# The first product of each iteration placed inside the older iteration's second product

## The chip, the cores and the metric

One of the eight cores of one Trainium2 chip runs the whole problem. The metric is the device time of one execution in microseconds (us). The engines are TensorE (PE in the profile; PEld are its weight loads), VectorE (DVE), ScalarE (ACT), GpSimd (POOL) and SyncE (SP, which here issues the DMAs).

## The reference

A softmax over 7 taps for each row and head, a causal mix of 7 neighbouring rows with these weights, and a feed-forward layer with `h * cos(h)` in the middle:

```python
w = exp(weight_gen - max); w = w / (sum(w) + 1e-09)      # (8, 4096, 8 heads, 7)
out = einsum('bshk,bskhg->bshg', w, x_unf)               # 7 rows of x, 192 columns
h = x @ w_in                                             # x = out as (32768, 192); w_in (192, 2048)
g = h * cos(h)
return g @ w_out                                         # w_out (2048, 192)
```

## The kernel before

The 32768 rows are cut into 64 blocks of 512. For each block GpSimd makes the mixed rows `xa` (`attention`, L257 products and L272 sums), TensorE transposes them (L316 for the steady part, L307 for the first blocks), ScalarE and GpSimd split them into a high part `x_hi` (L297) and a low part `x_lo` (L299). The feed-forward layer is computed in such high and low parts throughout.

The 2048 hidden columns are 8 "pairs" of 256. The main loop runs over i = 0 to 518, and i = 8b + pair names one block b and one pair. **One iteration** records:

- for i, the first product `x @ w_in` into one of 3 PSUM buffers `h`: `ffn_in_first` (L337, 6 slots of TensorE) and `ffn_in_second` (L354, 12 slots). The two halves of TensorE's rows write to two banks, and trade them between the two functions;
- for i − 1 and i − 2, the cosine and the split of g on ScalarE and VectorE: `act_turns` (L364), `dve_fraction` (L368), `act_cos` (L372), `dve_g` (L375), `act_hi` (L382), `dve_lo` (L386, which frees the h buffer);
- for j = i − 6, a part of the second product `g @ w_out`: `ffn_out` (L416), 16 slots with the high part `ghi` in f32, two transposes (L316), then 16 slots with the low part `glo` in bf16. Its `rest` picks a part of these: `False` all but the last 8 bf16 slots, `True` these last 8, `None` everything.

Two iterations in a row, j even and j odd, sum into one accumulator `acc`, and there is a single buffer for it (`ps_m`, `bufs=1`). After the odd one ScalarE copies it to SBUF (`evacuate`, L439; L443 where it holds no transposes), and only then may the next even one start. The same copy brings out the transposed rows.

Each engine runs its instructions in the order in which the code records them; the last loop of the kernel fixes that order. On ScalarE an iteration is L364, L382, L372, the split of x (L297), then the copy L439. Between `ffn_in_first` and `ffn_in_second`, and between the two iterations of an accumulator, `traded` puts a wait on SyncE's queue (shown in the profile under L283), so that the trade of banks is in order; L354 waits for it.

Every 32 iterations a softmax for 4 blocks runs beside this. Its exponential on ScalarE, with two loads of function tables, comes at `step == EXP`. In the iteration after it (`early_sums`) the products are recorded ahead of `act_hi`, and in the three after that (`EXP + 2 <= step <= EXP + 4`, i = 32, 33, 34, then 64, 65, 66 and so on) L337 stands between the two parts of `ffn_out`. In all other iterations `ffn_in_first` comes first, then the whole `ffn_out`, then `ffn_in_second`. For the first blocks (i = 5 and 13) a whole block is transposed in one go, and `ffn_out` comes before `ffn_in_first`. In iterations 1 to 8 parts of the weights are still being split (`two_parts`, L130 to L146), which takes h buffers too (`make_room`).

Of the kernel before, what the change touches and what calls it, by code (L numbers as in the profile page):

```python
# [43 lines left out]
def tile_softmax_conv_then_cos_ffn(  # L44
# [70 lines left out]
    def make_room():  # L115
        sizes = ps_h.tile([P, 2, CT], F32, name="h")
        bits = work.tile([P, 2, CW], F32, name="t1", tag="turn", bufs=TMP)
        room[:] = [(sizes[:, n, 0:CW].bitcast(I32), bits[:, n, :].bitcast(I32)) for n in range(2)]
# [68 lines left out]
    def softmax(r0, r1, eng, early=True, to=None):  # L187
        n = (r1 - r0) * H
        if r0 == 0:
            t = const.tile([P, n, K], F32, name="taps0")  # L190
        else:
            tile_ = work.tile([P, RW * H, K], F32, name="taps")
            t = tile_[:, 0:n, :]
        nc.sync.dma_start(out=t.rearrange("p a k -> p (a k)"), in_=g_v[:, :, r0 * H * K:r1 * H * K])
        for b in range(r0 // R, r1 // R):
            taps[b] = t.rearrange("p (r h) k -> p r h k", h=H)[:, b * R - r0:(b + 1) * R - r0]
        yield
        top_ = work.tile([P, RW * H], F32, name="top")
        top = top_[:, 0:n]
        nc.vector.tensor_reduce(out=top, in_=t, axis=AX.X, op=ALU.max)  # L200
        yield
        eng.tensor_tensor(
            out=t, in0=t, in1=top.unsqueeze(2).broadcast_to([P, n, K]), op=ALU.subtract)
        yield
        nc.scalar.activation(out=t, in_=t, func=AF.Exp)
        yield
        den_ = work.tile([P, RW * H], F32, name="den")
        den = den_[:, 0:n]
        if early:
            nc.vector.tensor_reduce(out=den, in_=t, axis=AX.X, op=ALU.add)  # L210
        else:
            add_taps(t, den)
        (nc.vector if early else nc.gpsimd).tensor_scalar(
            out=den, in0=den, scalar1=1e-9, scalar2=TWO_PI, op0=ALU.add, op1=ALU.mult)
        yield
        nc.vector.reciprocal(out=den, in_=den)
        yield
        m = 0 if to is None else to.shape[1]
        if m:
            eng.tensor_tensor(  # L220
                out=to, in0=t[:, 0:m], in1=den[:, 0:m].unsqueeze(2).broadcast_to([P, m, K]), op=ALU.mult)
        eng.tensor_tensor(
            out=t[:, m:], in0=t[:, m:], in1=den[:, m:].unsqueeze(2).broadcast_to([P, n - m, K]),
            op=ALU.mult)
        ready.update(range(r0 // R, r1 // R))
# [76 lines left out]
    def transpose_all(b):  # L302
        xa = mixed[b]
        tr = ps_h.tile([P, 2, CT], F32, name="h")
        for part in range(2):
            for r in range(R):
                nc.tensor.transpose(tr[:, part, r * P:(r + 1) * P], xa[:, r, columns(part)], ident)  # L307
        transposed.add(b)
        return tr
# [51 lines left out]
    def act_turns(i):  # L361
        t = work.tile([P, 2, CT], F32, name="turn", bufs=TMP)
        turns[i] = t
        nc.scalar.activation(out=t.bitcast(I32), in_=hs[i], func=AF.Identity, bias=0.25, scale=1.0)  # L364
# [27 lines left out]
    def ffn_out(j, rest=None):  # L392

        b, m = divmod(j, 2 * R)
        half, m = divmod(m, R)
        tp, s = divmod(m, 2)
        group = j // 2
        if s == 0 and not rest:  # L400
            accs[group] = ps_m.tile([P, 2, CT], F32, name="acc")
        acc = accs[group]
        whole = j + LAG >= N
        for lo in range(2):
            for c in range(2 * HALF):
                if rest is not None and rest != (lo == 1 and c >= HALF):
                    continue
                pair, n = divmod(c, 2)
                g = g_parts[b * NPAIR + half * HALF + pair][lo]
                fc = half * 2 * HALF + c  # L410
                for q in range(1 if whole else 2):
                    rs = slice(0, P) if whole else slice(q * D2, (q + 1) * D2)
                    bank = q ^ s
                    t = 2 * tp + bank
                    to, w = (acc[:, bank, 0:2 * D], wo) if lo == 0 else (acc[:, bank, 0:D], wo_b)
                    nc.tensor.matmul(  # L416
                        to, lhsT=g[rs, n, t * P:(t + 1) * P], rhs=w[rs, fc, :],
                        start=(lo == 0 and c == 0 and (whole or s == 0)),
                        stop=(lo == 1 and c == 2 * HALF - 1 and (whole or s == 1)),
                        skip_group_check=True)  # L420
            if lo == 0 and not rest:
                bt = group // R + 2
                if WHOLE < bt < NB:
                    transpose_row(bt, group % R, acc, s)
        if s == 0 and not whole and rest is not False:
            traded(acc)
# [60 lines left out]
    def until_mixed(b):  # L487
        while b not in mixed_all:
            next(bg)


    def all_of(*steps):
        steps = list(steps)
        while steps:
            steps = [s for s in steps if next(s, steps) is not steps]
# [71 lines left out]
    N = NB * NPAIR  # L567

    sm = sm2
    EXP = 6  # L570
    SOFTMAX = (0, 2, 3, EXP, 7, 12, 13)
    for i in range(N + LAG + 1):
        b, pair = divmod(i, NPAIR)
        j = i - LAG
        step = i % (SB * NPAIR) - (SB - 1) * NPAIR
        if step < 0 and i >= SB * NPAIR:
            step += SB * NPAIR
        if step == 0 and b + 4 < NB:
            r0 = (b + 4) * R
            sm = softmax(r0, min(r0 + RW, RPP), nc.gpsimd, early=False)  # L580
        busy = b + 4 < NB if step < NPAIR else b + 3 < NB
        exps = busy and step == EXP
        converts_now = converts.get(i, ())
        if converts_now:
            make_room()

        whole = None
        if pair == TR and b + 1 <= WHOLE:
            until_mixed(b + 1)
            whole = transpose_all(b + 1)  # L590
        if 0 <= j and j % (2 * R) == 0 and WHOLE < j // (2 * R) + 2 < NB:
            until_mixed(j // (2 * R) + 2)

        def products():
            if b < NB and pair == 0:
                assert b in transposed
            if whole is not None and j >= 0:

                ffn_out(j)
                ffn_in_first(i, whole)  # L600
            elif busy and EXP + 2 <= step <= EXP + 4:

                ffn_out(j, rest=False)
                ffn_in_first(i)
                ffn_out(j, rest=True)
            else:
                if i < N:
                    ffn_in_first(i, whole)
                if j >= 0:
                    ffn_out(j)  # L610
            if i < N:
                ffn_in_second(i)
            if j in stores:
                stores.pop(j)()
            if j >= 0:
                evacuate(j)


        early_sums = busy and step == EXP + 1
        if 0 <= i - 1 < N:  # L620
            act_turns(i - 1)
        if early_sums:
            products()
        if 0 <= i - 2 < N:
            act_hi(i - 2)
        all_of(*converts.pop(i - 1, ()))
        if exps:
            next(sm)
        now, later = [], []
        if not (busy and EXP + 1 <= step <= EXP + 3):  # L630
            now = list(splits)
            splits.clear()
        if whole is not None:
            t = work.tile([P, 2, CT], F32, name="part0", bufs=3)
            nc.scalar.copy(out=t, in_=whole)
            later.append(split(b + 1, t, slice(0, CT), nc.vector))
        if 0 <= i - 1 < N:
            dve_fraction(i - 1)
            act_cos(i - 1)
        for c in now:  # L640
            next(c)
        splits.extend(later)
        if 0 <= i - 2 < N:
            dve_lo(i - 2)
        if 0 <= i - 1 < N:
            dve_g(i - 1)
        for _ in range(4):
            for c in converts_now:
                next(c)
        all_of(*now)  # L650
        if i == N + LAG:
            break
        if not early_sums:
            products()
        load_weights(i)
        if step in SOFTMAX and step != EXP or NPAIR - 2 <= i < NPAIR + 1:
            next(sm, None)
        for _ in range(3 if i < 12 or i < 64 and i % 4 == 0 else 2):
            next(bg, None)
# [41 lines left out]
```

## Time and profile before

| | |
|---|---|
| median of 3 runs | 2300.2 us (2299.84 to 2303.83) |
| span of the profiled execution | 2300.3 us |
| TensorE busy | 2215.2 us |
| GpSimd, VectorE, ScalarE busy | 2002.3, 1905.0, 1897.5 us |
| DMA | 105.55 MB, mean 46 GB/s |

The profile is of one execution; its span lies within the runs' times. Its page gives totals by engine and slice, and its groups by line. The list of waits says who waited for whom, how long in total, how often and for how long at most. The timeline lists instructions in the order of time; in it "x2" are two slots that follow each other, and the number in brackets is the engine's idle time ahead and what ended it. Consecutive slots of TensorE overlap, so its steps are read from start to start.

### The profile page before, as it was taken

Reading aid. Unit: us, or ns where it says so; the run is one execution under the profiler, and the core shown is the slowest. Engines: PE = TensorE matmul, PEld = TensorE weight load, DVE = VectorE, ACT = ScalarE, POOL = GpSimd, SP = SyncE. Lnnn points to the kernel's source line nnn. Section 1 sums busy time; section 2 is a strip of 40 time slices with the busy share of each in tenths; the row PEclk is TensorE's granted clock in tenths of the full one; section 3 lists DMA queues with packets and bytes.
Section 4 is the critical chain, followed back from the end, with each engine's and each line's share of the span. In section 5 each row is a group of like instructions: output and inputs, shape, how many; then the busy total and the mean of one; then the engine's idle time right before and its main releaser. Section 6 shows DMA issues by size and latency. Waiting matters only on the chain.

```text
span 2300.3 us, 60609 instructions
## 1 busy us (share of the span) xinstructions
PE 2215.2 (96%) x26504; PEld 1993.6 (87%) x26504; DVE 1905.0 (83%) x1646; ACT 1897.5 (82%) x2131; POOL 2002.3 (87%) x1461
## 2 busy tenths in 40 slices
PE   3799999999999999999999999999999999999998
PEld 2588998889888888998989988898888889899897
DVE  7788888888888888888888888888888888888886
ACT  4588888888888888888888888888888888888885
POOL 8699989999999989989899899989989899899840
PEclk8799999999999999999999999999999999999999
DMA  6211221211211211211211212212211212212100
GB/s 154 56 43 40 50 51 33 58 41 34 58 39 44 50 40 44 50 49 34 58 33 43 58 31 52 50 32 52 50 41 42 58 26 50 57 26 52 33 9 22
DMA packets 25767, 105.55 MB, mean 46 GB/s; under 512 B 2734, under 2 KB 6566, under 8 KB 25502
## 3 DMA queue, kind: packets, MB, share of 16 engines
q1 hardware_dynamic: 25502, 101.67, 18.5%
q8 instruction: 208, 3.41, 0.6%
q14 instruction: 57, 0.47, 0.1%
HBM read 76.50 MB, written 25.17 MB: 44 GB/s over the span
## 4 chain that ended last, share of the span: by engine, by line
PE 56%; POOL 22%; ACT 11%; DVE 7%; issue 4%; DMA 0%; SPq 0%; POOLq 0%; ACTq 0%; DVEq 0%
PE acc L416 26%; PE h L354 19%; PE h L337 10%; POOL pr L257 6%; POOL xa L272 6%; DVE turn L368 3%; ACT part L439 3%; ACT turn L364 3%; POOL part L456 3%; DVE glo L386 2%; POOL x_lo L299 2%; POOL xa L257 2%; POOL fin L457 2%; ACT turn L372 2%; ACT ghi L382 1%
## 5 line engine op out<-in xcount | busy, mean ns | idle before, releaser
L368 DVE TENSOR_TENSOR turn<-h,turn 128x1024 f32<-128x1024 f32 x512 | 625.8, 1222 | 309.9 <-ACT turn L364 309.9
L416 PE MATMUL acc<-wo,ghi 64*128 64x384 f32 x8144 | 815.2, 336 | 16.6 <-ACT part L439 13.5
L416 PEld LDWEIGHTS acc<-wo,ghi 64*128 64x128 f32 x8144 | 739.2, 185 | 64.2 <-ACT part L439 26.7
L272 POOL TENSOR_TENSOR xa<-xa,pr 128x768 f32<-128x768 f32 (+1 forms) x384 | 704.0, 1833 | 0.7
L372 ACT ACTIVATE turn<-turn 128x1024 f32<-128x1024 f32 x512 | 543.7, 1062 | 181.0 <-DVE turn L368 177.7
L375 DVE SCALAR_TENSOR_TENSOR h<-h,turn 128x1024 f32<-128x1024 f32 x512 | 631.0, 1232 | 54.2 <-ACT turn L372 54.2
L364 ACT ACTIVATE turn<-h 128x1024 int32<-128x1024 f32 x512 | 525.6, 1027 | 165.0 <-PE h L354 164.2
L386 DVE TENSOR_TENSOR glo<-h,ghi 128x1024 bf16<-128x1024 f32 x512 | 622.4, 1216 | 9.9 <-ACT ghi L382 9.9
L257 POOL TENSOR_TENSOR pr<-xt,taps 128x768 f32<-128x768 f32 (+1 forms) x384 | 588.2, 1532 | 11.9
L382 ACT CAST ghi<-h 128x1024 fp32r<-128x1024 f32 x512 | 518.2, 1012 | 15.5 <-DVE h L375 15.5
L416 PE MATMUL acc<-wo_b,glo 64*128 64x192 bf16 x8144 | 435.6, 243 | 0.0
L456 POOL TENSOR_TENSOR part<-part,part 128x768 f32<-128x768 f32 x126 | 233.0, 1849 | 183.0 <-ACT part L439 156.7
L416 PEld LDWEIGHTS <-glo 64*128 64x128 bf16 x8144 | 333.8, 94 | 28.5 <-issue 13.7
L337 PE MATMUL h<-x_lo,wa_hi 64*128 64x512 f32 x1024 | 216.4, 410 | 37.0 <-DVE glo L386 28.4
L354 PE MATMUL h<-x_lo,wa_hi 64*128 64x512 f32 x1024 | 251.1, 478 | 0.6
L439 ACT COPY part<-acc 128x1024 f32<-128x1024 f32 x244 | 242.9, 996 | 0.0
L354 PE MATMUL h<-x_lo,wb_hi 64*128 64x512 f32 x1024 | 209.4, 397 | 0.0
L354 PE MATMUL h<-x_hi,wa_hi 64*128 64x512 f32 x1024 | 209.1, 396 | 0.0
L337 PE MATMUL h<-x_hi,wa_hi 64*128 64x512 f32 x1024 | 208.1, 394 | 0.0
L337 PE MATMUL h<-x_hi,wa_lo 64*128 64x512 f32 x1024 | 207.4, 392 | 0.0
L354 PE MATMUL h<-x_hi,wb_hi 64*128 64x512 f32 x1024 | 206.9, 391 | 0.0
L354 PE MATMUL h<-x_hi,wb_lo 64*128 64x512 f32 x1024 | 206.4, 391 | 0.0
(69 smaller groups left out, 2097.7 us busy)
## 6 DMA issues: line engine op xcount, KB each, us to landing
xt<-in_x_dram SPq DMA_DIRECT2D x62, 960.0 KB, 6.9
out_dram<-fin SPq DMA_DIRECT2D x63, 384.0 KB, 3.4
taps<-in_weight_gen_dram SPq DMA_DIRECT2D x15, 448.0 KB, 4.7
raw<-in_moe_w_out_dram SPq DMA_DIRECT2D x8, 384.0 KB, 4.2
raw<-in_moe_w_in_dram SPq DMA_DIRECT2D x10, 256.0 KB, 10.0
xt<-in_x_dram SPq DMA_DIRECT2D x1, 768.0 KB, 10.3
xt<-in_x_dram SPq DMA_DIRECT2D x1, 540.0 KB, 5.7
raw<-in_moe_w_in_dram SPq DMA_DIRECT2D x4, 128.0 KB, 5.6
```

The lines of the kernel that those rows point to most:

```text
L257: eng.tensor_tensor(out=dst.rearrange("p r (h g) -> p r h g", h=H), in0=xt[:, k + ra:k + rb, :].rearrange("p r (h g) -> p r h g", h=H), in ...
L272: eng.tensor_tensor(out=acc if k < K else xa, in0=acc, in1=old[:, ra:rb], op=ALU.add)
L337: nc.tensor.matmul(h[:, q, :], lhsT=w[rs, chunk(pair, q)], rhs=v[rs, q, :], start=(m == 0), stop=False, skip_group_check=True)
L354: nc.tensor.matmul(h[:, 1 - q, :], lhsT=w[rs, cs], rhs=v[rs, q ^ middle, :], start=False, stop=(m == len(prods) - 1), skip_group_check=True)
L364: nc.scalar.activation(out=t.bitcast(I32), in_=hs[i], func=AF.Identity, bias=0.25, scale=1.0)
L368: nc.vector.tensor_tensor(out=t, in0=hs[i], in1=t.bitcast(I32), op=ALU.subtract)
L372: nc.scalar.activation(out=t, in_=t, func=AF.Sin, bias=SIN_BIAS, scale=SIN_SCALE)
L375: nc.vector.scalar_tensor_tensor(out=hs[i], in0=hs[i], scalar=TWO_PI, in1=turns.pop(i), op0=ALU.mult, op1=ALU.mult)
L382: nc.scalar.copy(out=hi, in_=hs[i])
L386: nc.vector.tensor_tensor(out=lo, in0=hs.pop(i), in1=hi.bitcast(F32), op=ALU.subtract)
L416: nc.tensor.matmul(to, lhsT=g[rs, n, t * P:(t + 1) * P], rhs=w[rs, fc, :], start=(lo == 0 and c == 0 and (whole or s == 0)), stop=(lo == 1 ...
L439: nc.scalar.copy(out=part, in_=acc)
```

## The change

The condition of the branch that splits `ffn_out` is widened from three iterations in 32 to every iteration that has both a first product and an older second product:

```diff
-            elif busy and EXP + 2 <= step <= EXP + 4:
+            elif i < N and j >= 0:
 
                 ffn_out(j, rest=False)
                 ffn_in_first(i)
                 ffn_out(j, rest=True)
```

Only TensorE's order changes. On TensorE in the middle of the program, where an even iteration of a new accumulator begins (`acc` is the accumulator, `ghi` the high part of g, `xa` the mixed rows), the order before is this:

```order
L354 MATMUL h<-x_hi,wa_hi 128x512 x2
L354 MATMUL h<-x_hi,wb_hi 128x512 x2
L337 MATMUL h<-x_lo,wa_hi 128x512 [waits DVE_49,PE_49,Pool_49]
L337 MATMUL h<-x_lo,wa_hi 128x512
L337 MATMUL h<-x_hi,wa_lo 128x512 [waits Activation_49]
L337 MATMUL h<-x_hi,wa_lo 128x512
L337 MATMUL h<-x_hi,wa_hi 128x512 x2
L416 MATMUL acc<-wo,ghi 128x384 [waits Activation_49]
L416 MATMUL acc<-wo,ghi 128x384 x15
```

After the change, TensorE's rows at such a place are these:

```order
L354 MATMUL h<-x_hi,wa_hi 128x512 x2
L354 MATMUL h<-x_hi,wb_hi 128x512 x2
L416 MATMUL acc<-wo,ghi 128x384 [waits Activation_49]
L416 MATMUL acc<-wo,ghi 128x384 x15
L316 MATMUL acc<-ident,xa 128x64 [waits Pool_49]
```

The six slots of L337 no longer stand between the end of L354 and the first slot of the new accumulator, which waits for ScalarE.

The second place is on TensorE as well, at the end of an iteration's `ffn_out`, where the bf16 slots (`glo`, each with its weight load) meet L354, which waits for SyncE. Before:

```order
L416 LDWEIGHTS glo
L416 MATMUL acc<-wo_b,glo 128x192
L354 MATMUL h<-x_lo,wa_hi 128x512 [waits SP_sequencer_49]
L354 MATMUL h<-x_lo,wa_hi 128x512
L354 MATMUL h<-x_hi,wa_lo 128x512 x2
```

After the change the last of the first 8 bf16 slots, L337 and the first of the other 8 stand like this on TensorE:

```order
L416 LDWEIGHTS glo
L416 MATMUL acc<-wo_b,glo 128x192
L337 MATMUL h<-x_lo,wa_hi 128x512 [waits DVE_49]
L337 MATMUL h<-x_lo,wa_hi 128x512
L337 MATMUL h<-x_hi,wa_lo 128x512 x2
L337 MATMUL h<-x_hi,wa_hi 128x512 x2
L416 LDWEIGHTS glo
L416 MATMUL acc<-wo_b,glo 128x192
```

L337 now stands between the two halves of the bf16 slots; L354 follows 8 such slots behind it, where 16 f32 and 16 bf16 slots lay between.

## The prediction

> **What bounds the kernel now.** I read the page first: engine totals and the row of granted clock.
>
> ```profile
> span 2300.3 us, 60609 instructions
> PE 2215.2 (96%) x26504; PEld 1993.6 (87%) x26504; DVE 1905.0 (83%) x1646; ACT 1897.5 (82%) x2131; POOL 2002.3 (87%) x1461
> PEclk8799999999999999999999999999999999999999
> ```
>
> TensorE is busy for 96% of the span, and after the first slices it runs at full clock. Second, the list of waits: who still makes whom wait?
>
> ```profile
> ACT turn L364 <- PE h L354: 164.2, 230, 6.4
> PE h L337 <- DVE glo L386: 28.4, 22, 6.7
> PE acc L416 <- ACT part L439: 13.5, 29, 0.6
> PEld h L354 <- SPq L283: 5.1, 7, 0.8
> ```
>
> ScalarE waits for TensorE's second half of the first product (L354). TensorE waits for few things: a freed h buffer (L386), and, 29 times, a drained accumulator (L439). Third, the timeline of an ordinary stretch; columns are start, duration, engine, line, output and inputs, count, idle time before.
>
> ```profile
> 1003.93 1.03 ACT L364 ACTIVATE turn<-h 128x1024 int32<-128x1024 f32 x1 [0.57 <-PE h L354]
> 1004.40 1.60 PE L416 MATMUL acc<-wo,ghi 64*128 64x384 f32 x16
> 1004.99 1.23 DVE L368 TENSOR_TENSOR turn<-h,turn 128x1024 f32<-128x1024 f32 x1 [0.66 <-ACT turn L364]
> 1006.25 1.06 ACT L372 ACTIVATE turn<-turn 128x1024 f32<-128x1024 f32 x1 [0.39 <-DVE turn L368]
> 1007.22 1.00 ACT L439 COPY part<-acc 128x1024 f32<-128x1024 f32 x1
> 1007.72 0.42 PE L354 MATMUL h<-x_hi,wb_hi 64*128 64x512 f32 x2
> 1007.95 0.42 PE L337 MATMUL h<-x_lo,wa_hi 64*128 64x512 f32 x2
> 1008.64 1.60 PE L416 MATMUL acc<-wo,ghi 64*128 64x384 f32 x16
> ```
>
> One iteration is 1004.40 to 1008.64, 4.24 us, without a gap on TensorE; two of them (one accumulator) take 8.49. The second one starts a new accumulator at 1008.64. There is only one accumulator buffer, so ScalarE must have copied the old one out. That copy ended at 1007.22 + 1.00 = 1008.22: **0.42 us to spare**. The cover consists of two things between the last slot of the old accumulator and the first slot of the new one: L354 and the next first product, L337, from 1007.95 to 1008.64, 0.69 us. The change takes the second away.
>
> **The change part by part.** No instruction is added, and each engine but TensorE keeps its order; on SyncE too the word on h stays ahead of the word on the accumulator, the store and the load. What moves is L337, in every iteration from i = 6 on save i = 13 and the 45 that ran so already. For the price nothing has to be guessed: behind each exponential the kernel before already runs three iterations in the new order. These are its rows there.
>
> ```profile
> 1177.14 1.58 PE L416 MATMUL acc<-wo,ghi 64*128 64x384 f32 x16
> 1178.61 0.49 PE L416 MATMUL acc<-wo_b,glo 64*128 64x192 bf16 x8
> 1178.89 0.48 PE L337 MATMUL h<-x_lo,wa_hi 64*128 64x512 f32 x2
> 1179.67 0.50 PE L416 MATMUL acc<-wo_b,glo 64*128 64x192 bf16 x8
> 1179.96 0.47 PE L354 MATMUL h<-x_lo,wa_hi 64*128 64x512 f32 x2
> 1181.18 0.99 ACT L439 COPY part<-acc 128x1024 f32<-128x1024 f32 x1
> 1181.20 0.40 PE L354 MATMUL h<-x_hi,wb_hi 64*128 64x512 f32 x2
> 1182.23 1.67 PE L416 MATMUL acc<-wo,ghi 64*128 64x384 f32 x16 [0.63 <-ACT part L439]
> 1186.60 0.42 PE L337 MATMUL h<-x_lo,wa_hi 64*128 64x512 f32 x2
> 1186.82 1.02 ACT L364 ACTIVATE turn<-h 128x1024 int32<-128x1024 f32 x1 [0.76 <-PE h L354]
> 1189.14 1.06 ACT L372 ACTIVATE turn<-turn 128x1024 f32<-128x1024 f32 x1 [0.39 <-DVE turn L368]
> 1190.10 1.00 ACT L439 COPY part<-acc 128x1024 f32<-128x1024 f32 x1
> ```
>
> *The seams.* The rows from 1177.14 are an iteration in the new order with no wait in it. Its last L354 row starts at 1181.20, and such rows follow each other by 0.23 (1007.72 to 1007.95), so the next slot could start at 1181.43: 4.29 us, against 4.24. A second change between bf16 and f32 rows costs 0.05 an iteration. By itself that would be 0.10 a pair of iterations.
>
> *The handshake before L354.* L354 needs SyncE's word that L337 is through. Half of the bf16 slots now lie between them instead of the whole second product. The eight slots took 0.29 before L354 (1179.67 to 1179.96) and 0.28 before L337 (1178.61 to 1178.89), where no such word is awaited. So I take the handshake at nothing; if that cover were gone, it would cost what the seven waits for SPq average, 5.1 / 7 = 0.73 us.
>
> *The accumulator, the main term.* ScalarE's copy stands in its queue behind L364 and L372, and these wait in a chain that starts at L354: L364 (1186.82), L368 on VectorE, L372 (1189.14), copy (1190.10 to 1191.10). The ordinary rows have the same spacing: 1003.93, 1006.25, 1007.22. So the chain's length does not depend on the order of TensorE's slots, and its foot, L354, does not come earlier. After such a copy TensorE starts 0.05 to 0.06 later (1181.18 + 0.99 = 1182.17, then 1182.23). Take the accumulator that starts at 1182.23. Its first iteration ends where the next could start, at 1186.60. In the new order the second iteration needs 4.29, so TensorE would be ready at 1190.89; the accumulator is free at 1191.10 + 0.06 = 1191.16. **TensorE waits 0.27 us, and a pair of iterations takes 1191.16 − 1182.23 = 8.93 instead of 8.49: +0.44.** In this the first iteration holds 4.37 instead of 4.29, since weights are not loaded ahead of a waiting slot. What queues behind the waiting slot on TensorE is all of that iteration, L354 included, and so ScalarE's and VectorE's chain; the loop runs through the copy, and nothing makes the time good. Bounds for the pair: 8.59 if the wait vanished, 9.36 if it were 0.7 as behind an exponential; I take 8.93, which the rows give directly.
>
> *Behind an exponential* things are late already:
>
> ```profile
> 1163.57 1.03 ACT L364 ACTIVATE turn<-h 128x1024 int32<-128x1024 f32 x1
> 1172.32 1.67 PE L416 MATMUL acc<-wo,ghi 64*128 64x384 f32 x16 [0.29 <-ACT part L439]
> 1310.73 1.50 PE L416 MATMUL acc<-wo,ghi 64*128 64x384 f32 x14 [0.29 <-ACT part L439]
> ```
>
> The last two rows are the same slot of two blocks of 32 iterations, 138.41 apart. In each block ScalarE works without a pause from 1163.57 to the copy that frees 1172.32, 8.75; the accumulator before that one starts 0.06 after its own copy, so that pair takes 8.75 − 0.06 = 8.69. The next pair (1172.32 to 1182.23, 9.91) is in the new order already. The other 14 take 8.93: 125.0 + 8.69 + 9.91 = 143.6, or **+5.2 a block**. The block's wait for x_lo (9.6 us over 14 times, below) is hidden in this, since L337 comes 1.75 us later.
>
> ```profile
> PEld h L337 <- POOL x_lo L299: 9.6, 14, 0.7
> ```
>
> *The start* gains. L337 waits there for an h buffer while the second product, already possible, stands behind it:
>
> ```profile
> 76.44 0.80 PE L337 MATMUL h<-x_lo,wa_hi 64*128 64x512 f32 x2 [3.60 <-DVE glo L386]
> 84.13 1.22 DVE L368 TENSOR_TENSOR turn<-h,turn 128x1024 f32<-128x1024 f32 x1 [1.10 <-ACT turn L364]
> 86.63 0.50 PE L337 MATMUL h<-x_lo,wa_hi 64*128 64x512 f32 x2 [3.60 <-DVE glo L386]
> 93.83 1.23 DVE L368 TENSOR_TENSOR turn<-h,turn 128x1024 f32<-128x1024 f32 x1 [3.20 <-ACT turn L364]
> 95.19 1.00 POOL L146 TENSOR_TENSOR wo<-t,wo 128x384 fp32r<-128x384 f32 x1 [8.70 <-ACT wo L143]
> 96.33 0.80 PE L337 MATMUL h<-x_lo,wa_hi 64*128 64x512 f32 x2 [3.64 <-DVE glo L386]
> ```
>
> Most of three second products fits into the three waits, at most 3 × 3.6 = 10.8. VectorE's idle time before L368 limits the gain to 1.10 in the first and 3.20 in the next, 4.3; the third could give up to 3.6 more. GpSimd's wait (8.70) shrinks along. Between 0 and 9, I take 6.
>
> *The sum*, on the profiled span of 2300.3 (the median of the runs shown is 2300.2, so nothing has to be added): 15 blocks × 5.2 = 78; 8 pairs ahead of the first block × 0.44 = 3.5; start −6. **2376 us**, 3.3% slower.
>
> **The rivals.**
> (a) *Only the seams cost.* If the copy were not late, a pair would be 8.59: 250 × 0.10 = 25, less 6 and less 14 × 0.5 for x_lo: 2312. It needs the copy 0.27 earlier; L372 ahead of it in the same queue speaks against that. 5%.
> (b) *SyncE holds the handshake up.* SyncE also issues a load of x and a store for each of the 64 blocks of rows, some 0.6 us each:
>
> ```profile
> 138.21 0.61 SPq L462 DMA_DIRECT2D out_dram<-fin  x1
> ```
>
> If each stood between L337 and L354, 128 × (0.6 − 0.29) = 40 more: 2416. They are queued behind the handshake of their own iteration, some 2.5 us ahead of the next, and none of the 45 iterations in this order shows the wait. 5%.
> (c) *The clock falls.* A short stop of TensorE in each pair could set the clock back, as at the start:
>
> ```profile
> 60.00:104.00 44.00, 29.51 (x202) 23.22 (x200) 29.75 (x38) 21.92 (x34) 27.96 (x20) 0.68 0.19 50
> 112.00:2250.00 2138.00, 2117.23 (x25702) 1914.07 (x25700) 1793.44 (x1515) 1814.17 (x2022) 1913.52 (x1384) 1.00 0.18 43
> ```
>
> (PE, PEld, DVE, ACT and POOL busy, then the clock.) It is 0.68 where stops of 3.6 us come, but 1.00 through all 29 waits for the accumulator, of 0.29 and 0.63. If one iteration a block ran at half clock, 15 × 4.3 = 65 more: 2441. 3%. The Trainium skill, "TensorE: Matmul & The Clock Gate", section "A second HAM failure mode: psum-queue depth-cycling", reports a kernel that cycles its PSUM banks and stops so often for a moment that its clock goes back and forth between half and full. By that rule this rival would win; the 1.00 in the last row speaks against it here.
> (d) *Not slower:* the h buffer waits decide. The three waits at the start and the 14 for x_lo go (10.8 + 7), and the seams and the copy cost nothing: 2282. It turns faster only if a pair costs less than 18 / 250 = 0.07; the seams alone cost 0.10 in the rows. 2%.
> (e) *The edit does not do what it says:* the order of the built kernel shows L337 between the bf16 slots in ordinary iterations, so 1% for 2300.
>
> **How the numbers follow.** Forecast 84%, with its own spread: the pair 8.93 ± 0.05 gives ± 12, the start −9 to 0. That is about 2360 to 2394; a little wider, **2355 to 2395**, and rivals a to e, 16%, stay outside. A measurement of this kernel tells 0.2%, 4.6 us, from no change. Slower by more: forecast, a, b, c, so 96% after rounding; faster 2% (d); the same 2% (e, and a seam cost just balanced by the gains).
>
> **What would show it.** Waits of TensorE for the copy (L439) some 240 times, about 0.1 to 0.3 us each as idle time of its rows, every second iteration; pairs of 8.93; the copy always right behind L372; L364 still starting at once after L354; no more waits for x_lo, and the three waits for L386 at the start gone or short. Pairs of 8.6 without such waits would refute the main term; waits of L354 for SPq would point to (b), a clock below 1.00 to (c).

## The result, and the profile after

| | before | changed |
|---|---|---|
| median | 2300.98 us (4 runs, 2299.84 to 2303.83) | 2378.18 us (4 runs, 2377.26 to 2379.17) |
| span of the profiled execution | 2300.3 us | 2375.9 us |
| ratio | | 1.0329, interval 1.0316 to 1.0343 |

The page's totals of the changed kernel, and the chain of work that ended last (followed back from the last instruction), by engine:

```profile
PE 2281.4 (96%) x26504; PEld 1876.4 (79%) x26504; DVE 1907.9 (80%) x1646; ACT 1905.3 (80%) x2131; POOL 2004.8 (84%) x1461
PE 49%; ACT 28%; DVE 13%; issue 8%; POOL 1%; DMA 0%; SPq 0%; ACTq 0%; DVEq 0%; POOLq 0%
```

TensorE is "busy" for 96% as before, so this number shows nothing of the loss: a slot's modelled end overlaps the gap behind it. The busy time of the weight loads fell from 87% to 79% of the span. In the chain ScalarE and VectorE now hold 41%; before it was 18%:

```profile
PE 56%; POOL 22%; ACT 11%; DVE 7%; issue 4%; DMA 0%; SPq 0%; POOLq 0%; ACTq 0%; DVEq 0%
```

The list of waits of the changed kernel says where they came in:

```profile
ACT turn L364 <- PE h L354: 232.5, 231, 3.8
PEld acc L416 <- ACT part L439: 134.1, 243, 1.7
PE h L337 <- DVE glo L386: 24.6, 20, 6.3
PE acc L416 <- ACT part L439: 10.7, 16, 1.2
PEld h L354 <- SPq L283: 5.4, 7, 0.8
```

A wait of the accumulator's weight load for the copy L439 stands here 243 times; before it was 31 times:

```profile
PEld acc L416 <- ACT part L439: 26.7, 31, 1.1
```

The handshake over SyncE waits 7 times, as before. No wait of L337 for GpSimd's x_lo is left. Now one ordinary pair of iterations of the changed kernel on the timeline:

```profile
989.39 0.40 PE L354 MATMUL h<-x_hi,wb_hi 64*128 64x512 f32 x2
989.87 1.35 PEld L416 LDWEIGHTS acc<-wo,ghi 64*128 64x128 f32 x16 [0.53 <-ACT part L439]
989.87 1.68 PE L416 MATMUL acc<-wo,ghi 64*128 64x384 f32 x16
994.03 1.48 PEld L416 LDWEIGHTS acc<-wo,ghi 64*128 64x128 f32 x16
994.26 1.58 PE L416 MATMUL acc<-wo,ghi 64*128 64x384 f32 x16
994.47 1.03 ACT L364 ACTIVATE turn<-h 128x1024 int32<-128x1024 f32 x1 [0.96 <-PE h L354]
996.78 1.06 ACT L372 ACTIVATE turn<-turn 128x1024 f32<-128x1024 f32 x1 [0.39 <-DVE turn L368]
997.75 1.00 ACT L439 COPY part<-acc 128x1024 f32<-128x1024 f32 x1
998.31 0.40 PE L354 MATMUL h<-x_hi,wb_hi 64*128 64x512 f32 x2
998.80 1.68 PE L416 MATMUL acc<-wo,ghi 64*128 64x384 f32 x16
```

An accumulator starts at 989.87 and the next at 998.80: 8.93 us. TensorE was ready at 998.31 + 0.23 = 998.54; the copy ended at 998.75. So it stands for 0.26 us. The weight loads show a second cost: at 994.26, where nothing waits, the first load is 0.23 ahead of its slot (994.03); at 989.87, behind the wait, load and slot start together, and that iteration takes 4.39, against 998.54 − 994.26 = 4.28 for the next. Past the start the granted clock stays at 1.00 (sixth number behind the stretch's length):

```profile
112.00:2320.00 2208.00, 2174.68 (x25582) 1793.88 (x25581) 1787.97 (x1508) 1813.39 (x2013) 1909.11 (x1380) 1.00 0.17 42
```

Behind an exponential, and one block later, the accumulators start here:

```profile
1195.88 1.67 PE L416 MATMUL acc<-wo,ghi 64*128 64x384 f32 x16
...
1204.56 1.68 PE L416 MATMUL acc<-wo,ghi 64*128 64x384 f32 x16
...
1214.47 1.68 PE L416 MATMUL acc<-wo,ghi 64*128 64x384 f32 x16 [0.62 <-ACT part L439]
...
1348.11 1.68 PE L416 MATMUL acc<-wo,ghi 64*128 64x384 f32 x16
```

The two late pairs take 8.68 and 9.91, and the block from the second row to the last 143.55 us, against 138.41 before.

### The profile page after: what moved, and what is told of

The parts are those of the page before. It is cut to its first block, busy times and chain, and to the rows that moved or that the text cites. A ratio compares the mean times of both kernels' runs of the same rounds, so it can differ in the third digit from the quotient of the medians.

```text
span 2375.9 us, 60433 instructions
## 1 busy us (share of the span) xinstructions
PE 2281.4 (96%) x26504; PEld 1876.4 (79%) x26504; DVE 1907.9 (80%) x1646; ACT 1905.3 (80%) x2131; POOL 2004.8 (84%) x1461
## 4 chain that ended last, share of the span: by engine, by line
PE 49%; ACT 28%; DVE 13%; issue 8%; POOL 1%; DMA 0%; SPq 0%; ACTq 0%; DVEq 0%; POOLq 0%
PE acc L416 24%; PE h L354 16%; DVE turn L368 11%; ACT turn L364 10%; ACT part L439 10%; PE h L337 8%; ACT turn L372 5%; ACT ghi L382 1%; DVE glo L386 1%; ACT L205 1%; PE acc L316 1%; ACT L372 0%; DMA raw<-in_moe_w_in_dram 0%; POOL xa L272 0%; POOL pr L257 0%
## 5 line engine op out<-in xcount | busy, mean ns | idle before, releaser
L368 DVE TENSOR_TENSOR turn<-h,turn 128x1024 f32<-128x1024 f32 x512 | 626.8, 1224 | 381.5 <-ACT turn L364 380.4
L416 PE MATMUL acc<-wo,ghi 64*128 64x384 f32 x8144 | 832.8, 341 | 33.7 <-ACT part L439 10.7
L416 PEld LDWEIGHTS acc<-wo,ghi 64*128 64x128 f32 x8144 | 714.8, 185 | 162.0 <-ACT part L439 134.1
L364 ACT ACTIVATE turn<-h 128x1024 int32<-128x1024 f32 x512 | 525.9, 1027 | 234.2 <-PE h L354 232.5
L372 ACT ACTIVATE turn<-turn 128x1024 f32<-128x1024 f32 x512 | 543.4, 1061 | 180.4 <-DVE turn L368 177.0
L386 DVE TENSOR_TENSOR glo<-h,ghi 128x1024 bf16<-128x1024 f32 x512 | 622.3, 1215 | 10.4 <-ACT ghi L382 10.4
L416 PE MATMUL acc<-wo_b,glo 64*128 64x192 bf16 x8144 | 512.6, 244 | 0.0
L416 PEld LDWEIGHTS <-glo 64*128 64x128 bf16 x8144 | 307.4, 94 | 157.9 <-issue 140.8
L337 PE MATMUL h<-x_lo,wa_hi 64*128 64x512 f32 x1024 | 247.2, 477 | 29.6 <-DVE glo L386 24.6
L354 PE MATMUL h<-x_lo,wa_hi 64*128 64x512 f32 x1024 | 247.3, 477 | 0.6
L439 ACT COPY part<-acc 128x1024 f32<-128x1024 f32 x244 | 243.2, 997 | 0.3 <-PE acc L416 0.3
L299 POOL TENSOR_TENSOR x_lo<-part,x_hi 128x256 fp32r<-128x256 f32 x244 | 180.4, 742 | 50.8 <-ACT x_hi L297 50.8
L337 PE MATMUL h<-x_hi,wa_hi 64*128 64x512 f32 x1024 | 206.2, 396 | 0.0
L354 PE MATMUL h<-x_hi,wb_hi 64*128 64x512 f32 x1024 | 204.7, 394 | 0.0
L337 PE MATMUL h<-x_hi,wa_lo 64*128 64x512 f32 x1024 | 203.8, 392 | 0.0
L354 PE MATMUL h<-x_hi,wa_lo 64*128 64x512 f32 x1024 | 203.7, 392 | 0.0
L354 PE MATMUL h<-x_hi,wa_hi 64*128 64x512 f32 x1024 | 203.7, 392 | 0.0
```

Source lines behind the costliest of these rows:

```text
L337: nc.tensor.matmul(h[:, q, :], lhsT=w[rs, chunk(pair, q)], rhs=v[rs, q, :], start=(m == 0), stop=False, skip_group_check=True)
L354: nc.tensor.matmul(h[:, 1 - q, :], lhsT=w[rs, cs], rhs=v[rs, q ^ middle, :], start=False, stop=(m == len(prods) - 1), skip_group_check=True)
L368: nc.vector.tensor_tensor(out=t, in0=hs[i], in1=t.bitcast(I32), op=ALU.subtract)
L372: nc.scalar.activation(out=t, in_=t, func=AF.Sin, bias=SIN_BIAS, scale=SIN_SCALE)
L386: nc.vector.tensor_tensor(out=lo, in0=hs.pop(i), in1=hi.bitcast(F32), op=ALU.subtract)
L416: nc.tensor.matmul(to, lhsT=g[rs, n, t * P:(t + 1) * P], rhs=w[rs, fc, :], start=(lo == 0 and c == 0 and (whole or s == 0)), stop=(lo == 1 ...
```

## The experiments

The theory: the accumulator's copy sets the pace, because the new order takes L337 out of the time between L354 and a new accumulator's first slot. The main rival: each iteration in the new order pays by itself, at the seam or at the handshake. All ratios are to the kernel before, timed on the same chip in the same session.

**Only odd iterations in the new order** (their successor starts no accumulator):

```diff
-            elif busy and EXP + 2 <= step <= EXP + 4:
+            elif busy and EXP + 2 <= step <= EXP + 4 or i % 2 == 1 and i < N and j >= 0:
```

> New order in odd iterations only (those whose successor starts no accumulator; the three iterations behind an exponential stay as they were). Theory (the accumulator's copy is late because the new order takes L337 away from between L354 and a new accumulator's first slot): the cover stands again in front of every even iteration, so only a seam of 0.05 us an iteration is left: a pair 8.49 + 0.05 = 8.54, 240 pairs x 0.05 = 12, less about 3 at the start (only i = 7 gains there): 2310 us, and no waits of the accumulator's first slot for L439 but the 29 behind exponentials. Rival (each iteration in the new order pays by itself, through the seam or the handshake over SyncE): half of the 77 us, 2339 us.

Measured: 2307.6 us, ratio 1.0027 (1.0017 to 1.0036). The weight load's wait for the copy:

```profile
PEld acc L416 <- ACT part L439: 25.9, 30, 1.1
```

It is back at 30 times, against 31 in the kernel before. Odd iterations take 4.29 us, even ones 4.25. Half of the iterations are in the new order, and less than a tenth of the cost is there.

**Only even iterations in the new order** (`i % 2 == 0` in the same place).

> New order in even iterations only (those that start an accumulator). Theory: the cover is gone in front of each accumulator, and the loop L354 to L364, L368, L372, L439 to the next accumulator sets the pair at 8.93 whatever the odd iteration does: as dear as the whole change, 2374 to 2380 us, with about 240 waits for L439. Rival (each iteration in the new order pays by itself): half of the 77 us, 2339 us.

Measured: 2381.2 us, 1.0343 (1.0327 to 1.0358): the whole cost, with the other half of the iterations.

```profile
PEld acc L416 <- ACT part L439: 142.7, 243, 2.3
```

Iterations alternate between 4.25 and 4.68, so the pair is 8.93 again, although it holds one seam fewer: what the odd iteration saves, TensorE waits longer. A pair is as long as the loop through the copy: from L354 over L364, L368, L372 and L439 to the next accumulator. The rival's 2339 fits neither run.

**The copy ahead of the cosine.** TensorE's order is that of the changed kernel; on ScalarE the copy L439 moves ahead of L372 in odd iterations:

```diff
+        ahead = not early_sums and i % 2 == 1 and j >= 8 and i < N
...
             dve_fraction(i - 1)
+            if ahead:
+                products()
             act_cos(i - 1)
...
-        if not early_sums:
+        if not early_sums and not ahead:
             products()
```

> The changed kernel with its products recorded ahead of the cosine L372 in odd iterations from i = 15 on (not in the iteration behind an exponential), so that on ScalarE the copy L439 stands between L382 and L372. TensorE's order is that of the changed kernel. Theory (the copy is late only because it queues behind L372): the copy can start when the odd iteration's last slot is through, about 2.95 us behind the even iteration's L354 instead of 3.33, the accumulator is free 0.1 us before TensorE wants it, and a pair is 8.59: 250 x 0.10 for the seams, less 7 at the start and 7 for x_lo: 2312 to 2320 us, and waits for L439 only behind exponentials. Rival (TensorE's order itself costs): 2378 us as before.

Measured: 2306.8 us, 1.0022 (1.0013 to 1.0031). So 71 of the 77 us go away without a change to TensorE's order. TensorE and ScalarE in a pair:

```profile
1002.19 1.02 ACT L382 CAST ghi<-h 128x1024 fp32r<-128x1024 f32 x1
1004.03 1.01 ACT L439 COPY part<-acc 128x1024 f32<-128x1024 f32 x1 [0.82 <-PE acc L416]
1004.94 1.06 ACT L372 ACTIVATE turn<-turn 128x1024 f32<-128x1024 f32 x1
1004.96 0.39 PE L354 MATMUL h<-x_hi,wb_hi 64*128 64x512 f32 x2
1005.19 1.58 PE L416 MATMUL acc<-wo,ghi 64*128 64x384 f32 x16
```

The copy now waits for TensorE (0.82); it ends at 1005.04, and the accumulator's slot starts without a gap, 0.23 behind the last L354 row. The weight loads still wait for the copy, 183 times and 52.9 us in all, which was not expected; it costs the slots nothing that the pairs show. Pairs take 8.57: the two seams are all that is left. They cost 0.08 together, not 0.10; 250 × 0.02 = 5 us is about what the time lies below the lower end of what was expected.

**A tiny copy in front of the copy**, to lengthen the loop by a known amount, in the changed kernel and in the one before:

```diff
         part = work.tile([P, 2, CT], F32, name=f"part{half}", bufs=(3 if half == 0 else 2))
+        nc.scalar.copy(out=early, in_=early)
```

> The changed kernel with one tiny ScalarE copy (one element per partition) ahead of each accumulator copy L439, estimated at 0.2 us from the ScalarE copies of 256 and 1024 elements (0.39 and 1.00 us). Theory: the copy stands in the loop, so each of some 250 pairs grows by the whole filler: +50 us, 2428 us. Rival (seam or handshake pays, the copy has room): only the pairs behind an exponential grow, +6 us, 2384 us.

> The kernel before with the same tiny ScalarE copy ahead of each L439. Theory: 0.42 us to spare there swallow it in ordinary pairs; only the two late pairs of each of 15 blocks grow: +6 us, 2307 us, pairs still 8.49. If the room that I read from the timeline is not there: +50 us, 2351 us.

Measured: 2398.1 us (1.0417, 1.0402 to 1.0433) in the changed kernel, 20 us more than without the filler; 2306.3 us (1.0015, 1.0006 to 1.0025) in the one before. The first number missed both expectations. The filler (L438) and the copy (here L440) in the changed kernel:

```profile
1005.82 0.17 ACT L438 COPY early<-early 128x1 f32<-128x1 f32 x1
1005.90 1.01 ACT L440 COPY part<-acc 128x1024 f32<-128x1024 f32 x1
1006.96 1.68 PE L416 MATMUL acc<-wo,ghi 64*128 64x384 f32 x16 [0.18 <-ACT part L440]
...
1015.97 1.67 PE L416 MATMUL acc<-wo,ghi 64*128 64x384 f32 x16 [0.18 <-ACT part L440]
```

The filler lasts 0.17 but delays the copy by 0.08 only, since neighbouring ScalarE instructions overlap; the Trainium skill, "ScalarE: Activation LUTs", section "What ACT_TABLE_LOAD costs", gives about 93 ns for the overlap of activations that follow each other, and the rows, of a copy behind a copy, agree (0.17 − 0.08 = 0.09). A pair takes 9.01 instead of 8.93: the whole 0.08, 250 times, is 20. So the mechanism held and the estimate of the filler's size (0.2) was wrong. In the kernel before, ordinary pairs stay at 8.49.

**A larger dose in the kernel before:** one or two ScalarE copies of 256 elements of a tile `pad` at the same place.

> The kernel before with one ScalarE copy of 256 elements ahead of each L439, 0.29 us from start to next start by the x_hi rows (1031.64 to 1031.93). Theory: in the old order the accumulator is free 0.36 us before it is wanted (copy end 1008.22, 0.06 to TensorE, slot at 1008.64), so ordinary pairs stay at 8.49 and only the pairs behind exponentials grow, by 0.29 each: 15 x 2 x 0.29 = 9, 2310 us. Without that room: 250 x 0.29 = 72, 2374 us.

> The kernel before with two such copies, 0.58 us: more than the room of 0.36. Theory: TensorE now waits in every pair although its order is the old one: 0.58 - 0.36 = 0.22, and 0.10 more because the weights of a waiting slot are not loaded ahead: pairs of 8.81, 250 x 0.32 = 80, 2381 us, and waits for L439 some 240 times. If the wait needs the new order: 2318 us or less.

Measured: 2331.3 us (1.0125, 1.0105 to 1.0145) with one, 2431.9 us (1.0559, 1.0538 to 1.0579) with two. Both times missed what was expected, 2310 and 2381; the ordinary pairs tell the theories apart. With one, ordinary pairs are 8.50: the room takes 0.29. (Lines stand 2 or 3 lower here: L442 or L443 is the copy, L418 the accumulator's slot.)

```profile
1001.01 1.01 ACT L442 COPY part<-acc 128x1024 f32<-128x1024 f32 x1
1001.92 0.41 PE L339 MATMUL h<-x_hi,wa_hi 64*128 64x512 f32 x2
1002.07 1.36 PEld L418 LDWEIGHTS acc<-wo,ghi 64*128 64x128 f32 x16 [0.18 <-ACT part L442]
1002.16 1.59 PE L418 MATMUL acc<-wo,ghi 64*128 64x384 f32 x16
```

The weight load waits for the copy, and the slot itself (1002.16, behind 1001.92 by the usual 0.24) comes just in time. What was missed: in each block of 32 iterations six pairs around the softmax and the exponential grow, by 0.1 to 0.55 and by 1.9 us together, where two pairs and 0.6 were counted; 15 × 1.9 = 29 is the whole loss. Three of the six weren't late before (8.48 to 8.50), so the room isn't the same in every pair: in the kernel before, the copy ended only 0.23 ahead of the slot at one of them (878.53 and 878.76), where 0.42 to 0.46 is usual. The other places weren't followed up. With two, the loop closes in the old order too:

```profile
1002.59 0.39 ACT L440 COPY pad<-pad 128x256 f32<-128x256 f32 x1
1003.01 0.41 ACT L441 COPY pad<-pad 128x256 f32<-128x256 f32 x1
1003.32 1.01 ACT L443 COPY part<-acc 128x1024 f32<-128x1024 f32 x1
1004.38 1.66 PE L418 MATMUL acc<-wo,ghi 64*128 64x384 f32 x16 [0.17 <-ACT part L443]
```

The second pad waits for the first (0.42 instead of 0.29), so the dose is 0.73. Less the room of 0.36, plus 0.10 for weights that are not loaded ahead, that is 0.47; pairs are 8.93, 0.44 more, or 250 × 0.44 = 110 of the 130 us. The rest is in pairs around the exponentials. The wait does not need the new order; it needs the room to be used up.

**L337 directly ahead of L354**, in odd iterations, so that nothing covers the handshake:

```diff
+            elif i % 2 == 1 and i < N and j >= 0:
+                ffn_out(j)
+                ffn_in_first(i)
             else:
```

> In odd iterations L337 goes behind the whole second product, directly ahead of L354, so nothing covers the handshake over SyncE and there is no further seam between bf16 and f32 slots; even iterations as in the kernel before. Theory: the handshake's price without cover is what the start shows (L337's last row to L354 0.48 us instead of 0.23), 0.25 us in each odd iteration: 8.74 a pair, 60 us, 2355 to 2362 us, idle time of L354 put down to SPq in some 240 iterations. If the eight bf16 slots in the changed kernel hide nothing (the handshake costs nothing by itself): 2301 us.

Measured: 2368.5 us, 1.0291 (1.0273 to 1.0310). The list of waits, then one odd iteration:

```profile
PEld h L354 <- SPq L283: 130.8, 244, 0.8
```

```profile
1002.87 0.40 PE L337 MATMUL h<-x_hi,wa_hi 64*128 64x512 f32 x2
1003.37 0.50 PE L354 MATMUL h<-x_lo,wa_hi 64*128 64x512 f32 x2
1003.70 0.39 PE L354 MATMUL h<-x_hi,wa_lo 64*128 64x512 f32 x2
```

The handshake waits 244 times: 0.50 to L354 instead of 0.23, and 0.33 to the next row instead of 0.23, since the weights were not ahead. By these rows that is 0.37 an odd iteration; the pairs say 0.36 (8.85 instead of 8.49). The expected 0.25 left the second part out, so 2355 to 2362 was missed. In the changed kernel the eight bf16 slots hide all of this (7 waits, as before).

**The parts that gain, without the loss.** `start_only` puts iterations 6, 7 and 8 alone in the new order; `start_two` also takes the third iteration behind each exponential (even, and its accumulator late anyway) back to the old one:

```diff
-            elif busy and EXP + 2 <= step <= EXP + 4:
+            elif busy and EXP + 2 <= step <= EXP + 3 or 6 <= i <= 8:
```

(In `start_only` the upper bound stays `EXP + 4`.)

> The kernel before with the new order in iterations 6, 7 and 8 only. Theory: the gain at the start that the changed kernel shows, 7 us, alone: 2294 us. Rival (the gain there is given back by waits for GpSimd's mixing of the first blocks): 2300 us.

> As start_only, and the third iteration behind each exponential (i = 34, 66, ...), an even one, goes back to the old order, so that L337 stands in the time for which TensorE waits there for the copy (0.63 us of idle time in 15 places). Theory: the accumulator starts at the same time, and the 0.75 us of L337 and its seam behind it are saved: 15 x 0.73 = 11 us, 2283 us, faster than both kernels. Rival (L337 finds no h buffer there yet and waits for L386 instead): 2294 us or more.

Measured: `start_only` 2296.3 us, 0.9978 (0.9969 to 0.9987), 5.4 us faster; `start_two` 2286.4 us, **0.9932 (0.9920 to 0.9945)**, faster than both kernels, by 15 us than the one before. The third iteration behind an exponential in `start_two`:

```profile
1169.73 1.00 ACT L439 COPY part<-acc 128x1024 f32<-128x1024 f32 x1
1170.06 0.50 PE L337 MATMUL h<-x_lo,wa_hi 64*128 64x512 f32 x2
1170.83 1.45 PE L416 MATMUL acc<-wo,ghi 64*128 64x384 f32 x14
```

L337 now runs while the copy does, and the accumulator starts 0.10 behind the copy's end. From one end of L354 to the next that iteration takes 4.46 instead of 5.18: 15 × 0.72 = 11 us, of which 10 show.

## Why the prediction was right

Forecast 2376, range 2355 to 2395; measured 2378.2. The span grew by 75.6 us, the sum had 75.5. The prediction took span and time as one, but the profiled run of 2377.68 has a span of 2375.9, 1.8 less; on the span the forecast is off by 0.1. That it is so little is luck: the 15 blocks gave 77.7 instead of 78, the start gained 7.2 instead of 6, and the last pairs, which the sum left out, cost 1.6. That the main term is right is not luck; the experiments bear out its mechanism:

- *The accumulator.* The pair was predicted at 8.93 with a wait of 0.27; it is 8.93 with 0.26. That the new order exposes the copy is shown by the two halves (even iterations alone cost 80 us, odd ones alone 6), that the copy is late by its place behind L372 is shown by moving it, and that the loop passes a delay on in full is shown by the filler's 0.08.
- *The room before.* The prediction gave 0.42 to the end of the copy; less the 0.06 from there to TensorE it is 0.36. One pad of 0.29 fits in an ordinary pair, 0.73 does not. The 0.69 of L337 less 0.36, less the 0.05 by which the odd iteration is longer, is 0.28; the wait is 0.26.
- *The seams.* 0.05 an iteration: odd iterations alone show 4.29 against 4.25, and with the copy ahead a pair holds 0.08 for two. They are real but, in the changed kernel, hidden in the wait.
- *The handshake* taken at nothing: right, 7 waits as before. Its price without cover is 0.37, half of the 0.73 that the prediction gave for it.
- *Behind an exponential:* 8.69 and 9.91 were predicted, 8.68 and 9.91 came. The block was predicted at 143.6 and is 143.55. Over all 15 blocks the accumulator's slot goes from 203.50 to 2277.81 before and from 199.77 to 2351.79 after, which is 77.7 more.
- *The start.* The same accumulator slot (where the first of the 15 blocks starts) stands at 203.50 before and at 199.77 after:

```profile
203.50 1.67 PE L416 MATMUL acc<-wo,ghi 64*128 64x384 f32 x16 [0.28 <-ACT part L439]
```

```profile
199.77 1.68 PE L416 MATMUL acc<-wo,ghi 64*128 64x384 f32 x16
```

  It is 3.7 earlier, and 8 pairs × 0.44 = 3.5 were lost on the way, so the gain is 7.2 where 6 was taken. One detail was wrong: the three waits for L386 were to be gone or short. In the middle one TensorE, now ahead, waits longer than before (4.52 instead of 3.60):

```profile
75.48 0.50 PE L337 MATMUL h<-x_lo,wa_hi 64*128 64x512 f32 x2 [1.85 <-DVE glo L386]
84.48 0.50 PE L337 MATMUL h<-x_lo,wa_hi 64*128 64x512 f32 x2 [4.52 <-DVE glo L386]
92.34 0.50 PE L337 MATMUL h<-x_lo,wa_hi 64*128 64x512 f32 x2 [1.80 <-DVE glo L386]
```

  The reason given, waits that are filled, may be only a part of it. The granted clock is higher there too: the stretch up to the third of these iterations has 0.84, where the prediction's row of the kernel before has 0.68 (60 to 104).

```profile
60.00:95.00 35.00, 23.56 (x192) 18.19 (x192) 28.55 (x37) 20.74 (x32) 23.79 (x17) 0.84 0.24 63
```

  The slots are shorter with it: the first 16 `ghi` slots took 2.79 before and take 1.58 now.

```profile
77.85 2.79 PE L416 MATMUL acc<-wo,ghi 64*128 64x384 f32 x16
```

```profile
71.71 1.58 PE L416 MATMUL acc<-wo,ghi 64*128 64x384 f32 x16
```

  No run separates filled waits from the higher clock in the 7.2, so it is not shown that this term had the right reason, and that its size came near may be luck.

- *The sign by which to know it* was off in one place: the 240 waits do not stand as idle time of TensorE's slots but of its weight loads (134.1 us over 243), since a slot's modelled end hides 0.26 us.
- *The clock* did not fall in the 2208 us after the start, with 243 stops instead of 31.

The 5.4 us that `start_only` gains do not contradict the 7.2. The same slot as above stands in its profile at 196.36, 7.1 earlier than before, and its interval, 0.9969 to 0.9987, is 3 to 7 us:

```profile
196.36 1.67 PE L416 MATMUL acc<-wo,ghi 64*128 64x384 f32 x16 [0.28 <-ACT part L439]
```

What stays open: how much of the gain at the start is the clock, and why some pairs around the softmax have less room.

## What to carry to other kernels

Work that only fills the time between the last use and the next use of a single buffer is a cover with a size: measure it (here 0.36 us to spare, of the 0.69 that the moved work lasts) before moving it, and add to the loss what a stopped engine cannot prepare ahead (0.10 here). Where a buffer is released in the queue of an engine, look at what stands in front of the release there; one instruction's place moved 71 us. And where a kernel already runs the new order in a few places, look at its rows there: here they gave the pair of 8.93 and the handshake at nothing.

## What the runs showed of the hardware

- An accumulator's first slot that waits for the copy costs 0.10 us beyond the wait, since its weights are not loaded ahead (load and slot both start at 989.87): the iteration that it begins takes 4.39 instead of 4.28 us. L354's first slot shows the same behind the uncovered handshake (0.33 to the next instead of 0.23). When the copy comes just before the slot, only the weight load shows the wait (one pad).
- A ScalarE copy of one element per partition is recorded with 0.17 us, but delays the next instruction by 0.08. A copy of 256 elements delays it by 0.29 to 0.31, and by 0.42 where the next one reads its result (two pads).
- Some 240 stops of TensorE, 0.26 us in ordinary pairs and one every 8.93 us, left the granted clock at 1.00 from 112 to 2320 us.
